# Turning the first tiles uncentred through a diagonal matmul, with a new order of loads and slots, in a fused attention and two-layer network kernel

## The chip, the cores and the metric

One core of a Trainium2 chip. The metric is the device time of one execution in microseconds (us), median of several runs. All runs quoted here are in the fast state, with a mean granted TensorE clock of 0.991 or more. A profile's span is about 1.8 us shorter than the time of the same run (288.8 against 290.5 before the change), so spans are compared with spans and times with times. Engines: PE is the tensor engine, DVE the vector engine, ACT the scalar engine, POOL GpSimd, SP the sync engine, which here only issues transfers.

## The reference

Per batch (8) and head (8): `kv = kᵀ v`, `o = q kv`, normalised by its root mean square over the 64 columns of the head. The heads are laid side by side, which gives rows `x` of 512. Then a layer norm without shift, two matrix products with a relu between, and a residual:

```python
kv  = np.einsum('bhsd,bhse->bhde', k, v)
out = np.einsum('bhsd,bhde->bhse', q, kv)
rms = np.sqrt(np.mean(out * out, axis=-1, keepdims=True) + 1e-06)
x   = (out / rms * g_norm)                       # then to (batch, 576, 512)
xn  = (x - mu) / np.sqrt(var + 1e-06) * g_ln
y   = x + np.maximum(xn @ w_ch1, 0.0) @ w_ch2    # 512 -> 2048 -> 512
```

Inputs are float32, and the kernel computes its products in bf16. The factor 1/sqrt(var) is applied after the second product, which a relu allows. So a tile can enter the network as soon as its *centred* rows have been turned (transposed).

## The kernel before

The network's two products keep PE busy (131.6 and 129.1 of its 280.9 us). Everything else (k-v products, o, norms, turns) is planned into numbered *slots*: a slot is a group of about 16 matmuls of the first product, or 4 of the second, and `at(slot, fn)` issues work just ahead of it. In the traces below each engine works in the order of issue: a copy that is issued behind another operation on DVE also runs behind it (58.60 us, behind one of 57.93, in wait 2 below). A slot number therefore also fixes the place of an instruction in the queues of DVE, ACT and SP.

```python
def turn_q_dma(b):                     # q of a batch: reorder on DVE, turn by a DMA
    q_p = kv_in.tile([128, JJ, H, D], bf16, tag="qp", bufs=2)
    nc.vector.tensor_copy(q_p.rearrange("p j h d -> p h j d"), q_in[b % NB])
    q_t = qt_pool.tile([128, JJ, HP, 128], bf16, tag="qt", name="qt")
    nc.sync.dma_start_transpose(...)
    qts[b] = q_t

def kv_of(b):                          # 40 small matmuls, then two read-outs on ACT
    kv_ps = ps_m.tile([128, HP, D], f32, tag="misc", name="kv_ps")   # ps_m: ONE buffer
    ...
    nc.scalar.copy(kvp[:D, :, :D], kv_ps[:D])
    nc.scalar.copy(kvp[D:, :, D:], kv_ps[D:])

def turn(self, on_pe):                 # a tile's centred rows (xc) into xT
    if on_pe:
        tp = ps_m.tile([128, nK, 128], bf16, tag="misc", name="tp")  # the same buffer
        ...
    else:
        nc.sync.dma_start_transpose(dst, self.xc_t)

def plan_tile(s, make, turn_at, on_pe):
    at(s, first)          # o on PE, its square on ACT, the reduction on DVE
    at(s + 2, second)     # y, x, xc on DVE
    at(s + 6, third)      # variance on ACT
    at(turn_at, fourth)

# ... cut ... batch 1's tiles turn on PE, batch 2's by DMA
for j, s, tn in ((0, 24, 30), (1, 27, 34), (2, 31, 38), (3, 35, 42)):
    plan_tile(s, lambda j=j: main_tile(1, j), tn, True)
at(36, lambda: kv_of(2))
at(36.9, lambda: turn_q_dma(2))
for j, s, tn in ((0, 45, 51), (1, 49, 55), (2, 53, 61), (3, 57.5, 64)):
    plan_tile(s, lambda j=j: main_tile(2, j), tn, False)
```

At the start, batch 0's tiles 0 and 1 are centred in halves on DVE and then turned on PE:

```python
for c, xc in enumerate(halves_xc(0)):
    half_turn(0, c, xc, nc.scalar.copy)
t[1].red()
t[1].x_g()
xc1 = list(halves_xc(1))
```

## Time and profile before

| | before |
|---|---|
| time, median of the 4 runs beside the change | 290.5 us (290.46 to 290.83) |
| span of the profiled run | 288.8 us |
| PE busy | 280.9 us, 97% |
| network's first matmul | 14.95 us |
| last matmul | 284.86 us |

The waits of PE; the columns are what waited, for what, total us, how often, the longest. In this list a 0.2 us wait for a turned tile is the only one after batch 0:

```profile
PE even L225 <- DMA v_in<-in_v_dram: 1.5, 1, 1.5
PE p L198 <- DVE eps_sb L137: 1.2, 1, 1.2
PE tp L554 <- DVE xc L547: 0.4, 1, 0.4
PE p L413 <- DMA xT_blk<-xc: 0.2, 1, 0.2
```

Second, the timeline of 54 to 63 us, where k-v and q of batch 2 are made ready (start, length, engine, line, operation):

```profile
54.37 0.36 ACT L249 CAST kv_pack<-kv_ps 64x256 bf16<-64x256 f32 x1
...
55.45 0.82 DVE L203 COPY q_p<-q_in 128x2560 bf16<-128x2560 bf16 x1
...
55.76 0.39 PE L348 MATMUL tp<-identity,xc 128*128 128x128 bf16 x4
...
56.30 3.09 SPq L205 DMA_TRANSPOSE qt<-q_p  x1
...
62.45 0.39 PE L271 MATMUL o_ps<-kv_pack,qt 128*128 128x128 bf16 x4
```

ACT frees the single buffer at 55.1, before PE wants it at 55.76. The turn of q, issued at 56.30, lands at 61.18 (4.88 us) by the landing record, and PE uses it at 62.45. **There is 0.6 us of slack on the first and 1.3 us on the second, and no view prints slack.** It has to be read by setting two starts side by side.

The page's list of DMA queues (packets, MB, share of the 16 engines).

```profile
q1 hardware_dynamic: 38480, 17.91, 31.2%
q10 hardware_dynamic: 512, 0.72, 0.7%
q8 instruction: 18, 0.29, 0.4%
```

### The profile page before, as it was taken

The numbers are of one execution on the slowest core, as the hardware profiler recorded it, in microseconds if no ns is written. First come the engines' busy times: TensorE is split into PE (matmuls) and PEld (weight loads), VectorE is DVE, ScalarE is ACT, GpSimd is POOL, SyncE is SP. The second block draws the span as 40 slices with busy tenths as digits, with TensorE's granted clock in tenths as the row PEclk, the third lists the DMA queues.
The fourth block names the chain that finished last, engine by engine and source line by source line (L and its number), as shares of the span: only waits on it lengthen the run. The fifth ranks groups of instructions, "written<-read, shape, count | busy, mean of one in ns | idle before, by whom it ended". The sixth has DMA issues, their size and how long they took to land.

```text
span 288.8 us, 5753 instructions
## 1 busy us (share of the span) xinstructions
PE 280.9 (97%) x2295; PEld 157.9 (55%) x2295; DVE 149.8 (52%) x331; ACT 153.2 (53%) x333; POOL 41.0 (14%) x69
## 2 busy tenths in 40 slices
PE   7889999999999999999999999999999999999994
PEld 3579756995479644444444444444444444444444
DVE  5774119938897783764376935762578200220022
ACT  3477844985379733872288318921893066016400
POOL 8522510041005004100500032000000000000000
PEclk9999999999999999999999999999999999999999
DMA  7999999979788959996994189947203410230033
GB/s 214 199 206 205 198 190 195 214 112 193 138 173 101 194 108 157 202 159 120 157 217 68 39 152 219 155 84 149 56 18 64 101 36 0 48 81 19 0 73 75
DMA packets 67546, 36.76 MB, mean 127 GB/s; under 512 B 35516, under 2 KB 62524, under 8 KB 67520
## 3 DMA queue, kind: packets, MB, share of 16 engines
q0 software_dynamic: 28528, 17.76, 43.8%
q1 hardware_dynamic: 38480, 17.91, 31.2%
q10 hardware_dynamic: 512, 0.72, 0.7%
q8 instruction: 18, 0.29, 0.4%
q14 instruction: 8, 0.07, 0.1%
HBM read 36.71 MB, written 9.44 MB: 160 GB/s over the span
## 4 chain that ended last, share of the span: by engine, by line
PE 85%; DMA 5%; DVE 5%; ACT 2%; issue 1%; SPq 1%; DVEq 0%; POOLq 0%
PE p L413 41%; PE p L429 37%; PE o_ps L271 2%; DMA v_in<-in_v_dram 2%; DMA qt<-q_p 2%; PE kv_ps L246 2%; DMA xT_blk<-xc 1%; DVE ss L298 1%; ACT m L416 1%; DVE x_blk L322 1%; DVE y L303 1%; DVE o_sb L434 1%; PE p L198 1%; SPq L205 1%; ACT rms L308 0%
## 5 line engine op out<-in xcount | busy, mean ns | idle before, releaser
L413 PE MATMUL p<-xT_blk,w_sb 128*128 128x128 bf16 (+2 forms) x1024 | 131.6, 286 | 0.6 <-DMA xT_blk<-xc 0.2
L429 PE MATMUL p<-w_sb,m 128*128 128x512 bf16 (+2 forms) x608 | 129.1, 368 | 0.0
L416 ACT ACTIVATE m<-p 128x512 bf16<-128x512 f32 x144 | 85.2, 596 | 43.0 <-PE p L413 40.5
L413 PEld LDWEIGHTS <-w_sb 128*128 128x128 bf16 x1024 | 78.7, 98 | 44.9 <-issue 1.5
L429 PEld LDWEIGHTS <-m 128*128 128x128 bf16 x608 | 57.0, 98 | 62.0
L434 DVE SCALAR_TENSOR_TENSOR o_sb<-p,rstd,x_blk 128x512 f32<-128x512 f32 (+2 forms) x38 | 27.3, 720 | 52.2 <-PE p L429 41.2
L277 ACT ACTIVATE sq<-o_ps 128x512 f32<-128x512 f32 x35 | 20.9, 596 | 41.7 <-PE o_ps L271 41.7
L298 DVE TENSOR_REDUCE ss<-sq 128x8 f32<-128x512 f32 x35 | 23.7, 678 | 13.0 <-ACT sq L277 12.9
L340 ACT ACTIVATE dev<-x_blk,st_blk 128x512 f32<-128x512 f32 x36 | 25.7, 714 | 6.2 <-DVE st_blk L326 6.1
L332 DVE SCALAR_TENSOR_TENSOR xc<-x_blk,st_blk,g_ln_sb 128x512 bf16<-128x512 f32 x34 | 25.6, 752 | 1.2
L303 DVE TENSOR_TENSOR y<-o_ps,inv 128x512 f32<-128x512 f32 x33 | 22.8, 692 | 3.4 <-PE p L413 0.5
L322 DVE SCALAR_TENSOR_TENSOR x_blk<-y,g_norm_sb 128x512 f32<-128x512 f32 x33 | 22.8, 692 | 1.1
L315 DVE RECIPROCAL inv<-rms 128x8 f32<-128x8 f32 x36 | 7.2, 201 | 23.0 <-ACT rms L308 23.0
L422 DVE RECIPROCAL rstd<-rstd 128x4 f32<-128x4 f32 x9 | 1.6, 175 | 31.2 <-ACT rstd L421 31.1
L308 ACT ACTIVATE rms<-ss,eps_sb 128x8 f32<-128x8 f32 x36 | 10.7, 296 | 11.5 <-DVE ss L298 11.4
L98 POOL COPY gate<-qt 1x1 bf16<-1x1 bf16 x5 | 0.9, 177 | 106.4 <-DMA qt<-q_p 106.4
L271 PEld LDWEIGHTS <-qt 128*128 128x128 bf16 (+1 forms) x156 | 10.2, 100 | 8.1 <-issue 1.7
L271 PE MATMUL o_ps<-kv_pack,qt 128*128 128x128 bf16 (+1 forms) x156 | 13.7, 220 | 0.2
L198 PE MATMUL p<-fill_sb 128*128 128x512 bf16 x27 | 8.0, 448 | 1.2 <-DVE eps_sb L137 1.2
L340 ACT ACTIVATION_READ_ACCUMULATOR dev<-x_blk,st_blk 128x1 f32 x36 | 6.8, 189 | 0.0
L249 ACT CAST kv_pack<-kv_ps 64x256 bf16<-64x256 f32 x7 | 2.6, 366 | 7.7 <-PE kv_ps L246 7.7
L246 PEld LDWEIGHTS <-k_in 128*64 128x64 bf16 x280 | 5.0, 112 | 2.6 <-issue 2.5
(80 smaller groups left out, 110.5 us busy)
## 6 DMA issues: line engine op xcount, KB each, us to landing
out_dram<-o_sb SPq DMA_DIRECT2D x70, 128.0 KB, 2.4
w_sb<-in_moe_w_ch_dram POOLq DMA_DIRECT2D x8, 512.0 KB, 15.2
q_in<-in_q_dram POOLq DMA_DIRECT2D x7, 320.0 KB, 12.3
k_in<-in_k_dram POOLq DMA_DIRECT2D x7, 320.0 KB, 6.0
v_in<-in_v_dram POOLq DMA_DIRECT2D x7, 320.0 KB, 8.6
q_in<-in_q_dram POOLq DMA_DIRECT2D x8, 256.0 KB, 12.3
k_in<-in_k_dram POOLq DMA_DIRECT2D x7, 256.0 KB, 6.7
v_in<-in_v_dram POOLq DMA_DIRECT2D x7, 256.0 KB, 10.6
```

What stands on the lines that cost most here:

```text
L198: nc.tensor.matmul(p1, lhsT=fill_sb[:, :128], rhs=fill_sb, start=True, stop=True)
L271: nc.tensor.matmul(flat[rows, hp * 128:(hp + 1) * 128], lhsT=lhsT_of(hp), rhs=kvp[:, hp, :], start=True, stop=True)
L277: nc.scalar.activation(self.sq_t, self.o_ps, func=AF.Square)
L298: nc.vector.tensor_reduce(self.ss, self.sq_t, axis=AX.X, op=ALU.add)
L303: nc.vector.tensor_mul(self.y_t, self.o_ps, self.inv().to_broadcast([128, H, D]))
L322: nc.vector.scalar_tensor_tensor(x_blk[:, ts].rearrange("p (h d) -> p h d", h=H), in0=self.y_t, scalar=1.0, in1=g_norm_sb.to_broadcast([12 ...
L332: nc.vector.scalar_tensor_tensor(self.xc_t, in0=x_blk[:, self.ts], scalar=st[:, 1, self.ts:self.ts + 1], in1=g_ln_sb, op0=ALU.add, op1=ALU ...
L340: nc.scalar.activation(dev, x_blk[:, ts], func=AF.Square, bias=st[:, 1, ts:ts + 1], accum_out=st[:, 2, ts:ts + 1])
L413: nc.tensor.matmul(p1[:, i, :], lhsT=w1_sb[:, kk, de * 128:(de + 1) * 128], rhs=blk[2][:, kk, sl], start=(kk == 0), stop=(kk == nK - 1))
L416: nc.scalar.activation(m1[:, de0:de0 + per, sl], p1, func=AF.Relu)
L429: nc.tensor.matmul(p2[:, c0:c1], lhsT=m1s[b][:, de, ts * 128:(ts + 1) * 128], rhs=w2_sb[:, de, c0:c1], start=(de == 0), stop=(de == nDe - 1))
L434: nc.vector.scalar_tensor_tensor(o_sb[:, c0:c1], in0=p2[:, c0:c1], scalar=rstds[b][:, ts:ts + 1], in1=blks[b][0][:, ts, c0:c1], op0=ALU.mu ...
```

## The change

Its intent is to let PE enter the network's second stage earlier. Tiles 0 and 1 of batch 0 are turned before they are centred: a second matmul with the constant -1/512 and a diagonal of the row sums subtracts the mean in PSUM, and the layer norm's gain rides on the copies out. Tile 2's q and o go ahead of tile 1's turn. The upper half of q's rows is loaded in two pieces and w2 in five. The slots of batches 2, 3 and 4 are renumbered to suit; those of batch 1's main tiles and of batches 5 to 7 stay (`x_at` below equals the old `s + 2`). Cut to its core:

```diff
-    nc.gpsimd.dma_start(q_in[0][64:, :, :J], up(q, 0))
+    nc.gpsimd.dma_start(q_in[0][64:, :, :2], up(q, 0)[:, :, :2])
     load_w1(1)
     load_w1(2)
+    nc.gpsimd.dma_start(q_in[0][64:, :, 2:J], up(q, 0)[:, :, 2:])
     load_w1(3)
 ...
+        def turned(kk):
+            nc.tensor.matmul(tps[kk // 2][:, kk % 2], lhsT=flat[:, kk * 128:(kk + 1) * 128],
+                             rhs=identity, start=True, stop=False)
+
+        def centred(kk):
+            nc.tensor.matmul(tps[kk // 2][:, kk % 2], lhsT=mean_sb, rhs=self.diag,
+                             start=False, stop=True)
 ...
-    for c, xc in enumerate(halves_xc(0)):
-        half_turn(0, c, xc, nc.scalar.copy)
+    t[0].x_b()
+    t[0].mean_b(True)
     t[1].red()
-    t[1].x_g()
-    xc1 = list(halves_xc(1))
+    ...
+    t[0].turn_b()
+    turn_first(2, ps_m, "misc")
+    t[1].x_b()
+    t[1].mean_b()
 ...
-    for j, s, tn in ((0, 24, 30), (1, 27, 34), (2, 31, 38), (3, 35, 42)):
-        plan_tile(s, lambda j=j: main_tile(1, j), tn, True)
+    for j, s, x_at, tn in ((0, 24, 26, 30), (1, 27, 29, 34), (2, 31, 33, 38), (3, 35, 37, 42)):
+        plan_tile(s, lambda j=j: main_tile(1, j), tn, True, x_at)
-    at(36, lambda: kv_of(2))
-    at(36.9, lambda: turn_q_dma(2))
-    for j, s, tn in ((0, 45, 51), (1, 49, 55), (2, 53, 61), (3, 57.5, 64)):
+    at(37, lambda: kv_of(2))
+    at(37.8, lambda: turn_q_dma(2))
+    for j, s, tn in ((0, 46, 52), (1, 50, 56), (2, 54, 61), (3, 58, 64.5)):
 ...
+    for b, at_load, at_kv, at_q, at_o, step in (
+            (3, 48, 57, 57.7, 67, 4.7), (4, 68, 86, 87.3, 98.5, 4.5), ...
```

More of the change, by code (lines that the diff above doesn't have):

```diff
@@ L107, in load_w1, with load_w2 @@
             w1_sb[:, :, sl], moe_w_ch1[:, sl].rearrange("(ko p) n -> p ko n", p=128))
-    def load_w2(c):
-        n = nDe // 4
+    def load_w2(de0, de1):
         nc.gpsimd.dma_start(
-            w2_sb[:, c * n:(c + 1) * n, :],
-            moe_w_ch2[c * n * 128:(c + 1) * n * 128, :].rearrange("(ko p) n -> p ko n", p=128))
+            w2_sb[:, de0:de1, :],
+            moe_w_ch2[de0 * 128:de1 * 128, :].rearrange("(ko p) n -> p ko n", p=128))
     def pairs(t, hp0, hp1):
@@ L122 @@
     gate = consts.tile([1, 1], bf16)
+    mean_sb = consts.tile([128, 128], bf16)
+    gl_rows = consts.tile([nK, 128], f32)
+    four_sb = consts.tile([nK, nK], f32)
+    g_lnT_sb = consts.tile([128, nK], f32)
+    nc.vector.memset(mean_sb, -1.0 / Dm)
     nc.vector.memset(fill_sb, 0.0)
@@ L148 @@
                 ap=[[0, 4], list(g_norm.ap[0])]))
+    nc.sync.dma_start(gl_rows, bass.AP(tensor=moe_g_ln.tensor, offset=moe_g_ln.offset,
+                                       ap=[[128, nK], [1, 128]]))
     nc.vector.memset(kv_pack[0], 0.0)
@@ L155 @@
         nc.vector.memset(t, 0.0)
-    load_w2(0)
-    load_w2(1)
+    load_w2(0, 4)
+    load_w2(4, 8)
     for dst, src in ((q_in, q), (k_in, k), (v_in, v)):
         load(dst[1], src, 1)
-    load_w2(2)
-    load_w2(3)
+    load_w2(8, 10)
+    load_w2(10, 12)
+    load_w2(12, nDe)
     qts, held, blks, rstds, m1s, q_ps = {}, {}, {}, {}, {}, {}
@@ L284, in o_g, with x_b, mean_b @@
                                  rhs=kv_g[:, hp, :], start=True, stop=True)
-        def x_g(self):
+        def x_b(self):
+            _, st, _ = self.blk
+            self.i = self.inv().to_broadcast([128, H, D])
+            self.xb = work.tile([128, H, D], bf16, tag="xc", bufs=4, name="xb")
+            nc.vector.scalar_tensor_tensor(
+                self.xb, in0=self.og_ps, scalar=1.0, in1=self.i, op0=ALU.mult, op1=ALU.mult,
+                accum_out=st[:, 0, self.ts:self.ts + 1])
+        def mean_b(self, on_act=False):
+            self.diag = work.tile([128, 128], bf16, tag="diag", name="diag")
+            total = self.blk[1][:, 0, self.ts:self.ts + 1]
+            if on_act:
+                nc.scalar.activation(self.diag, identity, func=AF.Copy, scale=total)
+            else:
+                nc.vector.tensor_scalar_mul(self.diag, identity, total)
@@ new lines, in turn_b @@
+        def turn_b(self):
+            ts = self.ts
+            flat = self.xb.rearrange("p h d -> p (h d)")
+            tps = [ps_out.tile([128, 2, 128], f32, tag="ops", name="tp") for _ in range(2)]
+            def turned(kk):
[4 more added lines that the diff above has]
+                                 start=False, stop=True)
+            turned(0)
+            turned(2)
+            for kk in range(0, nK, 2):
+                centred(kk)
+                turned(kk + 1)
+                centred(kk + 1)
+            dst = self.blk[2][:, :, ts * 128:(ts + 1) * 128]
+            for kk in range(2):
+                nc.scalar.activation(dst[:, kk], tps[kk // 2][:, kk % 2], func=AF.Copy,
+                                     scale=g_lnT_sb[:, kk:kk + 1])
+            nc.vector.tensor_mul(dst[:, 2:], tps[1],
+                                 g_lnT_sb[:, 2:].rearrange("p (k o) -> p k o", o=1)
+                                 .to_broadcast([128, 2, 128]))
+            del self.xb, self.diag
@@ L287, in x_g @@
+        def x_g(self, mean=False):
             x_blk, st, _ = self.blk
             ts = self.ts
-            nc.vector.scalar_tensor_tensor(
-                x_blk[:, ts].rearrange("p (h d) -> p h d", h=H), in0=self.og_ps, scalar=1.0,
-                in1=self.inv().to_broadcast([128, H, D]), op0=ALU.mult, op1=ALU.mult,
-                accum_out=st[:, 0, ts:ts + 1])
+            x = x_blk[:, ts].rearrange("p (h d) -> p h d", h=H)
+            if mean:
+                self.i = self.inv().to_broadcast([128, H, D])
+                nc.vector.scalar_tensor_tensor(
+                    x, in0=self.og_ps, scalar=1.0, in1=self.i, op0=ALU.mult, op1=ALU.mult,
+                    accum_out=st[:, 0, ts:ts + 1])
+            else:
+                nc.vector.tensor_mul(x, self.og_ps, self.i)
@@ L293, in x_g @@
             nc.vector.tensor_scalar_mul(st[:, 1, ts:ts + 1], st[:, 0, ts:ts + 1], -1.0 / Dm)
-            del self.og_ps
+            del self.og_ps, self.i
         def red(self):
@@ L369, in rem_tile, with plan_tile @@
         return Tile(mms, blks["rem"], b // 2)
-    def plan_tile(s, make, turn_at, on_pe):
+    def plan_tile(s, make, turn_at, on_pe, x_at=None):
         box = []
@@ L393, in plan_tile @@
         at(s, first)
-        at(s + 2, second)
+        at(x_at or s + 2, second)
         at(s + 6, third)
@@ L426, in mm2_part @@
         for de in range(de0, de1):
-            if de % 4 == 0:
+            if (de - de0) % 4 == 0 and (de1 - de0 > 2 or ts % 2 == 0):
                 tick()
@@ L483 @@
     del gl_row
+    nc.vector.tensor_copy(four_sb, identity[:nK, :nK])
     qts[0] = qt_pool.tile([128, JJ, HP, 128], bf16, tag="qt", name="qt")
@@ L489 @@
     kv_b = KvFirst(HP - 1, HP, ((ps1, "p1"), (ps1, "p1")))
-    t = [main_tile(0, 0)] + [main_tile(0, i, *((ps1, "p1") if i == 1 else (ps2, "p2")))
+    t = [main_tile(0, 0)] + [main_tile(0, i, *((ps1, "p1"), (ps_m, "misc"), (ps2, "p2"))[i - 1])
                              for i in range(1, 4)]
@@ L536, with before_6 @@
     t[1].o_g(ps1, "p1")
-    fill(5, dead)
+    fill(1, dead)
+    glT = ps1.tile([128, nK], f32, tag="p1", name="glT")
+    nc.tensor.matmul(glT, lhsT=gl_rows, rhs=four_sb, start=True, stop=True)
+    fill(1, dead)
     del dead
-    t[0].x_g()
-    def halves_xc(i):
-        x_blk, st, _ = t[i].blk
-        for c in range(2):
-            cs = slice(c * Dm // 2, (c + 1) * Dm // 2)
-            xc = work.tile([128, Dm // 2], bf16, tag="xch", bufs=4, name="xc")
-            nc.vector.scalar_tensor_tensor(xc, in0=x_blk[:, i, cs], scalar=st[:, 1, i:i + 1],
-                                           in1=g_ln_sb[:, cs], op0=ALU.add, op1=ALU.mult)
-            yield xc
-    def half_turn(i, c, xc, copy):
-        tp = ps_out.tile([128, 2, 128], bf16, tag="ops", name="tp")
-        for kk in range(2):
-            nc.tensor.transpose(tp[:, kk, :], xc[:, kk * 128:(kk + 1) * 128], identity)
-        copy(t[i].blk[2][:, 2 * c:2 * c + 2, i * 128:(i + 1) * 128], tp)
-    for c, xc in enumerate(halves_xc(0)):
-        half_turn(0, c, xc, nc.scalar.copy)
-    t[1].red()
-    t[1].x_g()
-    xc1 = list(halves_xc(1))
+    t[0].x_b()
+    t[0].mean_b(True)
+    t[1].red()
+    nc.vector.tensor_copy(g_lnT_sb, glT)
+    del glT
+    t[1].root()
+    t[0].turn_b()
+    turn_first(2, ps_m, "misc")
+    t[1].x_b()
+    t[1].mean_b()
     def before_1():
-        turn_first(2, ps_m, "misc")
-        tp = ps2.tile([128, HP, 128], bf16, tag="p2", name="tp")
-        turn_groups(tp, 3, 0, H)
-        half_turn(1, 0, xc1[0], nc.scalar.copy)
         t[2].o()
-        half_turn(1, 1, xc1[1], nc.vector.tensor_copy)
+        t[1].turn_b()
         t[2].sq()
-        nc.scalar.copy(qts[0][:, 3], tp)
+        t[0].x_g()
         t[2].red()
         t[2].root()
-        del tp, xc1[:]
     def before_2():
         t[2].o_g(ps2, "p2")
-        t[2].x_g()
+        t[2].x_g(True)
         t[2].xc()
-    def before_5():
+        t[1].x_g()
+    def before_6():
         t[3].o()
@@ L596 @@
     at(2, before_2)
-    at(5, lambda: t[2].turn(True))
-    at(5.1, before_5)
+    at(5, lambda: (turn_first(3, ps_out, "ops", nc.vector.tensor_copy), t[2].turn(True)))
+    at(6, before_6)
     at(9.5, next_loads)
@@ L602 @@
         at(16 + i, lambda i=i: t[i].var())
-    at(20, lambda: (rstd_of(0), t.clear()))
+    at(20.3, lambda: (rstd_of(0), t.clear()))
     def q_start():
@@ L617, in q_turns @@
         del q_ps[1]
-    at(14.5, q_start)
-    at(19, q_turns)
+    at(15.6, q_start)
+    at(20, q_turns)
     at(22, lambda: kv_of(1))
-    for j, s, tn in ((0, 24, 30), (1, 27, 34), (2, 31, 38), (3, 35, 42)):
-        plan_tile(s, lambda j=j: main_tile(1, j), tn, True)
+    for j, s, x_at, tn in ((0, 24, 26, 30), (1, 27, 29, 34), (2, 31, 33, 38), (3, 35, 37, 42)):
+        plan_tile(s, lambda j=j: main_tile(1, j), tn, True, x_at)
     at(46, lambda: rstd_of(1))
-    at(36, lambda: kv_of(2))
-    at(36.9, lambda: turn_q_dma(2))
-    for j, s, tn in ((0, 45, 51), (1, 49, 55), (2, 53, 61), (3, 57.5, 64)):
+    at(37, lambda: kv_of(2))
+    at(37.8, lambda: turn_q_dma(2))
+    for j, s, tn in ((0, 46, 52), (1, 50, 56), (2, 54, 61), (3, 58, 64.5)):
         plan_tile(s, lambda j=j: main_tile(2, j), tn, False)
-    plan_tile(62, lambda: rem_tile(1), 69, False)
+    plan_tile(62.5, lambda: rem_tile(1), 69, False)
     at(78, lambda: rstd_of(2))
-    for b in range(3, B):
-        s = 32 * b
-        at(47 if b == 3 else s - 60,
-           lambda b=b: load_batch(b, qts[b - 1][:1, J, HP - 1, 127:],
-                                  *([blks[2][2][:1, nK - 1, 511:]] if b == 4 else [])))
-        d = -41 if b == 3 else -45
-        at(s + d + (1 if b < 5 else 0), lambda b=b: kv_of(b))
-        at(s + d + 1.7, lambda b=b: turn_q_dma(b))
+    for b, at_load, at_kv, at_q, at_o, step in (
+            (3, 48, 57, 57.7, 67, 4.7), (4, 68, 86, 87.3, 98.5, 4.5),
+            *((b, 32 * b - 60, 32 * b - 45, 32 * b - 43.3, 32 * b - 32, 5) for b in range(5, B))):
+        at(at_load, lambda b=b: load_batch(b, qts[b - 1][:1, J, HP - 1, 127:],
+                                           *([blks[2][2][:1, nK - 1, 511:]] if b == 4 else [])))
+        at(at_kv, lambda b=b: kv_of(b))
+        at(at_q, lambda b=b: turn_q_dma(b))
         for j in range(J):
-            o = s + d + (11 if b == 3 else 13) + 5 * j
+            o = at_o + step * j
             plan_tile(o, lambda b=b, j=j: main_tile(b, j), o + 6, False)
         if b % 2:
-            plan_tile(s - 14, lambda b=b: rem_tile(b), s - 8, False)
-        at(s + 14, lambda b=b: rstd_of(b))
+            o = 32 * b - (12 if b == 3 else 14)
+            plan_tile(o, lambda b=b: rem_tile(b), o + 6, False)
+        at(32 * b + 14, lambda b=b: rstd_of(b))
     at(32 * B + 14, lambda: rstd_of("rem"))
@@ L654 @@
     p2s += [ps2.tile([128, Dm], f32, tag="p2", name="p2") for _ in range(2)]
-    for de0, de1 in ((0, nDe // 2), (nDe // 2, nDe * 3 // 4)):
+    for de0, de1 in ((0, 8), (8, 10), (10, 12), (12, nDe)):
         for ts in range(4):
-            mm2_part(0, ts, p2s[ts], de0, de1)
-    for ts in range(4):
-        p2 = p2s[ts]
-        p2s[ts] = None
-        mm2_part(0, ts, p2, nDe * 3 // 4, nDe)
-        finish(0, ts, p2)
-        del p2
+            p2 = p2s[ts]
+            mm2_part(0, ts, p2, de0, de1)
+            if de1 == nDe:
+                p2s[ts] = None
+                finish(0, ts, p2)
+            del p2
     del blks[0], m1s[0]
```

## The prediction

> **What bounds the kernel now.** I began with the page: busy times, slices, waits of the tensor engine (PE).
>
> ```profile
> PE 280.9 (97%) x2295; PEld 157.9 (55%) x2295; DVE 149.8 (52%) x331; ACT 153.2 (53%) x333; POOL 41.0 (14%) x69
> ...
> PE   7889999999999999999999999999999999999994
> ...
> DMA  7999999979788959996994189947203410230033
> ...
> L413 PE MATMUL p<-xT_blk,w_sb 128*128 128x128 bf16 (+2 forms) x1024 | 131.6, 286 | 0.6 <-DMA xT_blk<-xc 0.2
> ```
>
> PE is never idle for long after slice 4 (7.2 us each). No change can gain much unless it removes PE work, and this one removes next to none. So I looked for places where PE starts a matmul later than the one before allows. The chain of waits shows three clusters.
>
> First, batch 0's tiles 0 and 1, until their two-layer network can run:
>
> ```profile
> 13.10 1.08 PE p L198 x5
> ...
> 14.52 0.37 ACT xT_blk L555
> 14.92 0.37 ACT xT_blk L555
> ...
> 16.76 0.50 DVE xc L547
> ...
> 17.30 0.29 PE tp L554 x2
> ...
> 18.36 0.94 PE p L413 x14
> ...
> 24.57 0.30 ACT rms L308
> 24.87 0.49 ACT m L416
> ...
> 25.41 2.85 PE p L413 x48
> ```
>
> Columns: start, length, what. Five filler matmuls, then mean, centring in halves, transposes and copies; tile 1's turn is waited for; a relu (L416) behind a square root costs 0.24 us more near 25 us.
>
> Second, the first v of batch 1. The timeline shows it in GpSimd's and PE's rows:
>
> ```profile
> 39.00 0.68 POOL L94 DMA_DIRECT2D q_in<-in_q_dram  x1 [1.88 <-DMA v_in<-in_v_dram]
> ```
>
> GpSimd issued nothing until v had landed; the landing record of that transfer says 38.47 us. PE starts the k-v products of batch 1 at 38.72. Following on its matmul of 38.39 without a wait would be 38.39 + 0.213 (512 columns) + 0.096 (the usual switch between these shapes, seen at batches 3 to 6) = 38.70. So v and PE arrive within 0.03 us of each other. **This decides what the head start is worth.**
>
> Third, the border of batches 2 and 3:
>
> ```profile
> 105.65 0.82 DVE L203 COPY q_p<-q_in 128x2560 bf16<-128x2560 bf16 x1
> ...
> 106.53 3.10 SPq L205 DMA_TRANSPOSE qt<-q_p  x1
> ...
> 109.69 1.26 SPq L352 DMA_TRANSPOSE xT_blk<-xc  x1
> ...
> 111.63 0.40 PE L271 MATMUL o_ps<-kv_pack,qt 128*128 128x128 bf16 x4
> ...
> 112.25 1.02 PE L413 MATMUL p<-xT_blk,w_sb 128*128 128x512 bf16 x4 [0.23 <-DMA xT_blk<-xc]
> ```
>
> The sync queue issues the turn of batch 4's q (3.10 us) ahead of the turn of batch 3's last tile, whose xc was ready at 102.4. PE waits for both: from start to start, [...] 0.27 us ahead of L271 and 0.40 ahead of L413.
>
> [...] x48 in 2.69 us is 56 ns, x12 in 2.59 us is 216. [...] batch 0's loads and weights land one after another, 13.3 to 44.8 us, at 199 to 207 GB/s in every 4 us stretch from 8 to 36 us. [...] 128x512 from PSUM takes 0.69 us.
>
> **The change part by part.**
>
> *Diagonal turn, tiles 0 and 1.* Removed per tile: the -mean (0.15 us), two half centrings (0.88), four transposes, two copies of 128x256 (0.37 each). Added per tile: a 128x128 diagonal (estimate from the 128x256 and 128x512 copies, 0.37 and 0.59: 0.26 us on the scalar engine, ACT[...]), eight matmuls of 56 ns, two ACT copies of 128x128 (0.26 each), one DVE product of 128x256 (0.37). Worked through: the uncentred tile 0 is there at 13.43, diagonal 13.75, eight matmuls end 14.3. But ACT then does tile 1's root (waits for the reduction, 14.15) 14.2 to 14.5 and the two copies, to 15.0. PE meanwhile turns q's third group, which needs the first half of the upper q: landing 13.31 (w1's first quarter) + half of the 2.31 us that the whole took = about 14.5. So the network's first matmul comes at 15.0 to 15.3; it was 14.95, with a further gap to 15.34. **No gain on tile 0**, though q's third turn (0.48 us with its switches) is already behind.
> Tile 1: uncentred 15.7, diagonal 15.95, matmuls to 16.7; its copies wait for tile 0's relu (16.1 to 16.7) and end 17.2. Its 16 matmuls end at about 18.15 against 19.14: 1.0 us ahead, of which 0.48 is q's fourth turn, put off to slot 5.
>
> *Debt.* x itself is needed for variance and residual, so two 0.69 us products return on DVE. Tile 0's stands ahead of tile 2's reduction, so tile 2's root ends at 18.96, its relu behind at 19.5, and PE, ready at 19.3, loses 0.3. Tile 3's o, now one slot later with its q copied by DVE, avoids most of the 0.24 us at 25.11.
> Head start at the second product's first slot: 1.0 - 0.48 - 0.3 + 0.2 = 0.4 us at best, 0.1 to 0.2 less if upper q's half lands late.
>
> *At batch 1's v.* The bytes ahead of v are the same, less none, plus 2 KB of g. Unless the halves load faster, v lands at 38.47 again and the 0.2 to 0.4 us become a wait: **worth 0 to 0.1.**
>
> *w2's third quarter in two pieces.* It landed at 41.475, 81 ns of excess ahead of PE's 41.52; half of it lands about 1.5 us sooner: gain 0.07.
>
> *Later slots.* The instruction order of the changed kernel has batch 3's last turn ahead of batch 4's q turn on the sync queue, and batch 4's first o 2.5 slots later (two matmul slots of 0.86 us). q, ready by about 112.0, then meets a PE that needs it at about 112.8. Both gaps close: 0.27 + 0.40 = 0.67, less some 0.04 of switches: 0.63. At 82.79 PE waited 0.21 for batch 3's q (landed 83.06); the copy of q moves one slot, but DVE's o_sb now fills two of its 0.37 us waits for the square root, so q is ready nearly as early while PE needs it 0.9 us later: 0.1.
>
> Sum: 0.05 + 0.07 + 0.63 + 0.1 = 0.85; I take 0.1 to 0.15 off for a new small wait somewhere. 290.46 - 0.7 = **289.75 us**.
>
> **Rivals.** (1) *The head start counts in full*: v lands sooner because the small q pieces flow better (the whole upper q took 2.31 us for 256 KB, the same size of batch 1 1.39). Another 0.3 to 0.9 us: about 289.1. Against: the queue is full throughout. (2) *The start gets slower*: upper q's half lands after 14.6 and now stands ahead of the first slot; every 0.1 us beyond the head start of 0.3 counts fully: 290.2 to 290.6. For: landings of neighbours scatter by up to 1 us. (3) *DVE becomes the bound* in batch 2 to 4: slots begin one later, DVE is 8 to 9 tenths full there; if batch 4's q copy slips by 1 us, PE waits again at the new place and the 0.63 shrink to 0.2: 290.2. Against: batch 3's tiles stand 4.7 slots apart (over 4 us), DVE had idle moments at 95 us (1.28).
>
> **Range and chances.** All terms are tenths of 290 us; 2% is 5.8 us, more than every wait named here together. Range 289.1 to 290.7; faster by over 2% 0.01, within 0.98, slower 0.01.
>
> **What would show it.** The first 128x128 matmul of L471 (was L413) near 15.1, tile 1's last near 18.2; a wait on DMA v_in ahead of the k-v products near 38.7, unchanged in time; no gap for xT_blk near 111; q's turn for batch 4 behind the tile's turn on the sync queue. Wrong if k-v of batch 1 starts over 0.3 us before 38.7 (rival 1) or after it (rival 2), or if PE still waits for qt near 113.

Its sum came to 0.05 + 0.07 + 0.63 + 0.1 = 0.85 us, and 0.7 after the allowance. An estimate for a diagonal on DVE came from no trace (it took 0.25 us after the change). That a new order of loads leaves v's landing in place was not shown beforehand; the result bore it out (38.47 us before, 38.49 after). The 0.27 and 0.40 us are given as *excess*, defined with the waits below, in which 512 columns count 0.213 us. The 0.04 of switches is the author's estimate. The 1.5 us for half of w2's quarter is half of the 3.0 us from v's landing (38.47) to the quarter's own (41.48). The scatter of landings is read off the same trace: up to 55 us, pieces of 256 KB landed 1.30 to 2.55 us after the load before them.

## The result, and the profile after

| | before | after |
|---|---|---|
| time, median of 4 runs | 290.5 us (290.46 to 290.83) | 293.8 us (293.39 to 294.26) |
| ratio of the fast runs | | 1.0112 (95%: 1.0092 to 1.0131) |
| span of the profiled run | 288.8 us | 291.6 us |
| last matmul | 284.86 us | 287.65 us |

Ratios here and below are the mean time of one kernel's fast runs over that of the other's in the same rounds, so not quite the ratio of the medians. The change made the kernel 1.1% slower, with every run outside the predicted range of 289.1 to 290.7. The page's PE row now has an 8 that was a 9 (the ninth digit, 58 to 66 us):

```profile
PE 281.0 (96%) x2302; PEld 158.4 (54%) x2302; DVE 150.3 (52%) x335; ACT 153.9 (53%) x334; POOL 43.3 (15%) x71
...
PE   8889999989999999999999999999999999999994
```

To place the loss I took from each trace the first matmul of every stage of the network (P1 is the first product, P2 the second), and from the differences the length of each stage:

| stage | before, us | after, us | difference |
|---|---|---|---|
| up to the first matmul of batch 0's P1 | 14.95 | 15.53 | +0.58 |
| P1 of batch 0 | 18.03 | 17.54 | -0.49 |
| P2 of batch 0 | 16.11 | 16.01 | -0.10 |
| **P1 of batch 1** | **16.27** | **19.14** | **+2.87** |
| P2 of batch 1 | 15.79 | 15.79 | 0.00 |
| P1 of batch 2 | 14.86 | 15.43 | +0.57 |
| P2 of batch 2 | 16.24 | 15.38 | -0.86 |
| P1 of batch 3 | 14.48 | 14.71 | +0.23 |
| the rest, to the last matmul | 158.13 | 158.12 | -0.01 |
| sum | 284.86 | 287.65 | +2.79 |

The start, where the change does its work, comes out even: +0.58 - 0.49 - 0.10 = -0.01. The border of batches 2 and 3 gains 0.63. **The loss is in P1 of batch 1, where only slot numbers changed**, and 0.57 more in P1 of batch 2. The busy times of that stretch, before and then after (stretch, its length, busy time of PE, PEld, DVE, ACT and POOL with their instruction counts, clock, DMA share, GB/s), say that PE stood idle there, at full clock (1.00 in both), with the same amount of work on DVE and ACT:

```profile
49.00:65.40 16.40, 16.40 (x319) 16.16 (x317) 10.46 (x22) 14.10 (x33) 3.86 (x7) 1.00 0.89 168
```

```profile
49.00:68.20 19.20, 16.71 (x318) 16.18 (x316) 10.53 (x22) 14.29 (x32) 1.68 (x4) 1.00 0.63 129
```

PE's waits after the change:

```profile
PE o_ps L279 <- DMA qt<-q_p: 1.8, 1, 1.8
...
PE tp L406 <- ACT kv_pack L258: 0.7, 1, 0.7
PE p L471 <- ACT m L474: 0.6, 1, 0.6
PE tp L192 <- DMA q_in<-in_q_dram: 0.6, 1, 0.6
```

Below I give waits as *excess*: the time from one matmul's start to the next one's, less its columns at the pace of the trace. In before, undisturbed matmuls of 512 columns start 216 ns apart (12 in 2.59 us) and those of 128 columns 56 ns apart (48 in 2.69 us), so 384 columns more take 160 ns, and 512 count 213 ns. By this measure a start that waits for nothing has an excess of 3 ns, or about 100 at some switches (96 to k-v). It is a little more than what the list above says. The first two, in the timeline:

```profile
54.93 0.68 DVE L356 TENSOR_REDUCE ss<-sq 128x8 f32<-128x512 f32 x1
...
55.64 0.30 ACT L366 ACTIVATE rms<-ss,eps_sb 128x8 f32<-128x8 f32 x1
...
55.85 0.35 ACT L257 CAST kv_pack<-kv_ps 64x256 bf16<-64x256 f32 x1
...
56.63 0.38 PE L406 MATMUL tp<-identity,xc 128*128 128x128 bf16 x4 [0.67 <-ACT kv_pack L258]
...
57.93 0.75 DVE L390 SCALAR_TENSOR_TENSOR xc<-x_blk,st_blk,g_ln_sb 128x512 bf16<-128x512 f32 x1
...
58.60 0.82 DVE L211 COPY q_p<-q_in 128x2560 bf16<-128x2560 bf16 x1
...
59.45 3.06 SPq L213 DMA_TRANSPOSE qt<-q_p  x1
```

**Wait 1 (0.84 us).** k-v of batch 2, one slot later, starts at 54.13 (before: 53.20). Its read-outs now queue on ACT behind a variance and a square root and run from 55.85 (before: 54.37). The turn of batch 1's tile needs the same single PSUM buffer, and PE stands.

**Wait 2 (1.99 us).** The copy of batch 2's q on DVE, moved from slot 36.9 to 37.8, has crossed slot 37, where y, x and xc of batch 1's last tile are issued. It runs behind them, at 58.60 instead of 55.45. The turn is issued 3.15 us later, lands at 66.16, and batch 2's first o waits. The chain of waits (start, length, what) runs exactly through these steps:

```profile
58.60 0.83 DVE q_p L211
59.45 6.71 DMA qt<-q_p
66.16 0.05 issue
66.20 0.40 PE o_ps L279 x4
```

The turn took 6.71 us; the same turn took 4.88 before. That 1.83 us is as important as the late issue: at its usual length the turn would have landed at 59.45 + 4.88 = 64.33, and PE was ready at about 64.2.

**Wait 3 (0.79 us).** The page calls it a wait of L471 for a relu (ACT m L474). The timeline at 92 us shows what it was:

```profile
92.22 0.47 POOL L98 COPY gate<-xT_blk 1x1 bf16<-1x1 bf16 x1 [6.63 <-DMA xT_blk<-xc]
92.23 1.03 PE L471 MATMUL p<-xT_blk,w_sb 128*128 128x256 bf16 x8 [0.62 <-ACT m L474]
```

GpSimd waits for the turned last tile of batch 2 (xT) to gate a load. It gets it at 92.22, and PE starts 0.01 us later on the same tile: the wait is the turn's, and the relu named is only the last of PE's other conditions. This turn was issued at 87.57 and so took 4.65 us; before, issued at 85.71, it was there at 88.36, after 2.65 us.

So two turns took about 2 us longer than the same ones before. What lies in their time is in the packet records of the DMA queues: queue 8, "instruction", moves one packet of 16,384 bytes 18 times in each of the two profiles, on average 246 recorded matmuls and weight loads of PE apart (some records can be missing). One of them starts at 64.13 us and takes 0.93 us, 2.0 us ahead of the landing of q's turn, and one starts at 90.05. Before, they started at 62.17 and 89.20, each about 1 us after the turn had landed. This gave the theory that the experiments test.

The start: PE's first eight new matmuls end at 14.56, and then it waits for the first piece of upper q, which landed at 15.11 us:

```profile
14.34 0.22 PE L321 MATMUL tp<-diag,mean_sb 128*128 128x128 bf16 x1
...
15.16 0.44 PE L192 MATMUL tp<-identity,q_in 64*64 64x64 bf16 x16 [0.60 <-DMA q_in<-in_q_dram]
...
15.53 0.68 PE L471 MATMUL p<-xT_blk,w_sb 128*128 128x128 bf16 x9
```

And the border of batches 2 and 3: the tile's turn now stands ahead of q's on the sync queue, and no wait is left there.

```profile
107.75 1.29 SPq L410 DMA_TRANSPOSE xT_blk<-xc  x1
110.72 3.05 SPq L213 DMA_TRANSPOSE qt<-q_p  x1
```

### The profile page after: what moved, and what is told of

The parts are those of the page before. It is cut to its first block, busy times and chain, and to the rows that moved or that the text cites. A ratio compares the mean times of both kernels' runs of the same rounds, so it can differ in the third digit from the quotient of the medians.

```text
span 291.6 us, 5773 instructions
## 1 busy us (share of the span) xinstructions
PE 281.0 (96%) x2302; PEld 158.4 (54%) x2302; DVE 150.3 (52%) x335; ACT 153.9 (53%) x334; POOL 43.3 (15%) x71
## 4 chain that ended last, share of the span: by engine, by line
PE 82%; DMA 6%; DVE 5%; ACT 3%; POOL 1%; issue 1%; DVEq 0%; POOLq 0%
PE p L487 41%; PE p L471 37%; DMA q_in<-in_q_dram 3%; PE o_ps L279 2%; DMA qt<-q_p 2%; PE kv_ps L254 2%; ACT m L474 1%; DVE x_blk L380 1%; DVE y L361 1%; DVE ss L356 1%; DVE o_sb L492 1%; DVE xc L390 1%; ACT sq L285 1%; ACT rms L366 0%; POOL v_in L130 0%
## 5 line engine op out<-in xcount | busy, mean ns | idle before, releaser
L471 PE MATMUL p<-xT_blk,w_sb 128*128 128x128 bf16 (+2 forms) x1024 | 131.6, 286 | 1.0 <-ACT m L474 0.6
L474 ACT ACTIVATE m<-p 128x512 bf16<-128x512 f32 x144 | 85.2, 596 | 50.1 <-PE p L471 48.2
L471 PEld LDWEIGHTS <-w_sb 128*128 128x128 bf16 x1024 | 78.5, 98 | 45.2 <-issue 1.4
L480 DVE RECIPROCAL rstd<-rstd 128x4 f32<-128x4 f32 x9 | 1.6, 175 | 36.9 <-ACT rstd L479 36.9
L254 PE MATMUL kv_ps<-v_in,k_in 128*64 128x64 bf16 x280 | 5.8, 197 | 0.0
```

Source lines behind the costliest of these rows:

```text
L254: nc.tensor.matmul(kv_ps[hh * D:hh * D + D, hp, :], lhsT=k_in[b % NB][:, h, j, :], rhs=v_in[b % NB][:, h, j, :], start=(j == 0), stop=(j = ...
L471: nc.tensor.matmul(p1[:, i, :], lhsT=w1_sb[:, kk, de * 128:(de + 1) * 128], rhs=blk[2][:, kk, sl], start=(kk == 0), stop=(kk == nK - 1))
L474: nc.scalar.activation(m1[:, de0:de0 + per, sl], p1, func=AF.Relu)
```

## The experiments

**Theory A**: the loss comes from two slot numbers of batch 2, k-v (36 to 37) and q's copy (36.9 to 37.8); the new start is worth about nothing. **Rival**: the loss comes from the new start (more work on DVE, new loads), or from k-v alone. **Theory E**: a turn by DMA that an instruction packet falls into lands about 2 us late, and where the packets fall depends on how many instructions PE has executed. Its rival is that those turns were slowed by the loads beside them.

| kernel | what it is | median (range), us | ratio to before |
|---|---|---|---|
| after | | 293.8 (293.39 to 294.26) | 1.0112 |
| q_back | after, batch 2's q copy at its old slot | 291.1 (290.56 to 291.52) | 1.0016 (0.9999 to 1.0033) |
| kv_back | after, batch 2's k-v at its old slot | 294.01 (293.88 to 294.07) | 1.0116 (1.0101 to 1.0131) |
| kvq_back | both | 290.1 (289.7 to 290.54) | 0.9982 (0.9966 to 0.9998) |
| front_only | new start and loads, all later slots old | 291.99 (291.79 to 292.19) | 1.0047 (1.0032 to 1.0062) |
| before_split | before, 32 PE instructions more | 291.81 (291.61 to 292.35) | 1.0034 (1.0016 to 1.0053) |
| before_period | before, 252 more | 291.78 (291.25 to 292.65) | 1.0044 (1.0021 to 1.0066) |
| after_shift | after, 150 more | 291.85 (291.18 to 292.82) | 1.0035 (1.0017 to 1.0054) |
| late_only | before, batch 3's tile spacing, its remainder tile and batch 4's slots as in after | 290.18 (289.88 to 291.14) | 0.9986 (0.9964 to 1.0009) |
| late_kv23 | late_only, batch 1's k-v a slot later | 290.04 (289.89 to 290.59) | 0.9984 (0.9969 to 0.9999) |
| kvq_swap | kvq_back, upper q's first piece ahead of w1 | 289.69 (289.27 to 289.95) | 0.9962 (0.9945 to 0.998) |
| kvq_swap_kv23 | kvq_swap, batch 1's k-v a slot later | 289.37 (289.23 to 290.03) | 0.9957 (0.9939 to 0.9976) |

Every kernel gave the reference's result, with 4 runs each. They ran in three groups, each beside its own 7 runs of before (medians 290.54, 290.5 and 290.62).

### Undoing the two slot numbers: q_back, kv_back, kvq_back

```diff
-    at(37, lambda: kv_of(2))
-    at(37.8, lambda: turn_q_dma(2))
+    at(36, lambda: kv_of(2))            # kv_back, kvq_back
+    at(36.9, lambda: turn_q_dma(2))     # q_back, kvq_back
```

> The changed kernel, with only the DVE copy of batch 2's q (and its DMA turn) put back from slot 37.8 to 36.9, so that it again stands ahead of y, x and xc of batch 1's tile 3; k-v of batch 2 stays at slot 37. Theory A (that place in DVE's order is the loss): the copy starts near 55.5 us instead of 58.6, the turn lands 61 to 62, PE's wait of 1.99 us for qt near 64 is gone, the 0.84 us behind the k-v copies stays: 291.8 us. Rival B (a slot's shift of everything, or a fetch of instructions that happens to meet the turn): the wait stays, 293.5 to 294.

> The changed kernel, with only k-v of batch 2 put back from slot 37 to 36; q's copy stays late. Theory A: PE no longer waits 0.84 us at the turn of slot 38 (the PSUM buffer that k-v and that turn share is read out a slot earlier), but it then comes to batch 2's first o 0.84 us earlier and waits that much longer for q, which lands as before near 66.1: 293.7 us, worth 0.1 at most. Rival B (the two waits are separate and add): 293.0 us.

> The changed kernel, with both put back (k-v of batch 2 at slot 36, its q at 36.9), tiles of batch 2 to 4 and the start as changed. Theory A: both waits are gone, 0.84 + 1.99 us: 290.9 us, and lower by up to 0.6 if the wait of 0.79 us near 91 goes too. Rival B: no less than 293.

In q_back the copy of q is back in its place and the wait for q is gone. Wait 1 remains as it was (0.83 us). Its timeline:

```profile
55.51 0.82 DVE L211 COPY q_p<-q_in 128x2560 bf16<-128x2560 bf16 x1
...
56.36 3.06 SPq L213 DMA_TRANSPOSE qt<-q_p  x1
56.62 0.38 PE L406 MATMUL tp<-identity,xc 128*128 128x128 bf16 x4 [0.67 <-ACT kv_pack L258]
```

Moving k-v alone back removes wait 1 (the turn starts at 55.72 in kv_back) and gains nothing by the end. PE arrives earlier at the wait for q, which grows from 1.99 to 2.51 us:

```profile
55.72 0.39 PE L406 MATMUL tp<-identity,xc 128*128 128x128 bf16 x4
...
59.32 0.82 DVE L211 COPY q_p<-q_in 128x2560 bf16<-128x2560 bf16 x1
...
60.17 3.65 SPq L213 DMA_TRANSPOSE qt<-q_p  x1
65.82 0.40 PE L279 MATMUL o_ps<-kv_pack,qt 128*128 128x128 bf16 x4 [2.34 <-DMA qt<-q_p]
```

So wait 2 takes back 0.52 of the 0.84 us, not all of it as expected: P2 of batch 1 begins at 67.84, 0.38 ahead of after. That rest is lost at wait 3, which grows from 0.79 to 1.78 us and has an instruction packet in its turn:

```profile
PE o_ps L279 <- DMA qt<-q_p: 2.3, 1, 2.3
PE p L471 <- DMA xT_blk<-xc: 1.6, 1, 1.6
```

With both back, the time is 290.1, 3.7 us below after. **Theory A holds**: one digit for q is worth 2.7 us (293.8 to 291.1), and the one for k-v 1.0 us once q is out of the way (291.1 to 290.1), but nothing before, with wait 3 mixed in. In the profiles P1 of batch 1 shrinks by 2.00 us in q_back and by 0.87 more in kvq_back, as A has it; wait 3 is 0.45 us in q_back and 0.66 in kvq_back, at 88.59. Kvq_back's four runs fall into two pairs, 289.7 and 290.5, and the profiled one is of the slower pair, so what makes the faster pair faster isn't shown. Two waits in a row need not add: here the second absorbed more than half of the first.

### The new start alone: front_only

Here the new start and the w2 pieces stay, and everything from slot 14 on is as before.

> Only the change of the start (diagonal turn, tile 2 ahead of tile 1, upper q in halves, w2 in smaller pieces); every slot from 14 on as in the kernel before. Theory A (the start as such neither gains nor loses, since q's half lands at 15.1 and v of batch 1 at 38.5): 290.5 us, k-v of batch 1 near 38.75. Rival C (the start itself costs, by the later first slot of 0.58 us): 291.0. Rival D (the start gains): 290.1.

The expectation of 290.5 missed by 1.5 us. It was right about the start: k-v of batch 1 begins at 38.62 (before: 38.72), and P1 of batch 2 at 81.04 (before: 81.15). But then comes a wait of 1.35 us that neither A nor its rival knows, at 88.59, for the turned last tile of batch 2, which was issued at 85.61 (before: 85.71):

```profile
90.03 0.18 POOL L98 COPY gate<-xT_blk 1x1 bf16<-1x1 bf16 x1 [6.78 <-DMA xT_blk<-xc]
90.04 3.65 PE L471 MATMUL p<-xT_blk,w_sb 128*128 128x256 bf16 x32 [1.18 <-DMA xT_blk<-xc]
```

The turn took 4.42 us instead of 2.65, with an instruction packet at 87.02 in its middle. The same slots and almost the same times, but seven more matmuls in the program: this is where theory E comes from.

### Moving the instruction packets: before_split, before_period, after_shift

PE runs 18 dummy matmuls of 512 columns at the start. Splitting them adds PE instructions without adding columns, and nothing else in the program changes:

```diff
-        for _ in range(n):
-            nc.tensor.matmul(p1, lhsT=fill_sb[:, :128], rhs=fill_sb, start=True, stop=True)
+        for i in range(n):
+            parts = 8 if i < eighths else 2 if i < eighths + halves else 1
+            w = 512 // parts
+            for c in range(0, 512, w):
+                nc.tensor.matmul(p1[:, c:c + w], lhsT=fill_sb[:, :128], rhs=fill_sb[:, c:c + w], ...)
-    fill(18)
+    fill(18, halves=16)              # before_split:  16 matmuls and 16 weight loads more
+    fill(18, eighths=18)             # before_period: 126 and 126 more
+    fill(18, eighths=10, halves=5)   # after_shift:   75 and 75 more
```

> The kernel before, with 16 of the 18 filler matmuls at its very start (512 columns each, on zeros, while k and v load) written as two of 256 columns: the same array time, 32 more PE instructions, nothing else. Theory E (a 16 KB packet of PE's own instructions, one per some 250 of them, [...] 14 more instructions moved it from just after batch 2's last turn, 89.2 us, to into it): the packet comes near 87 to 88 us, that turn lands 1 us late or more, PE waits 0.5 to 1.4 us near 89: 291.0 to 291.9 us. Rival F (that wait comes from the changed schedule or from DVE): 290.5 us, no wait near 89.

> The kernel before, with all 18 filler matmuls of its start written as eight of 64 columns: 252 more PE instructions[...], the same columns. Theory E (what counts is where in the work the packets of instructions fall, not how many instructions there are): they fall nearly where they fell in the kernel before, the one near 89 us after batch 2's last turn; no wait of 1 us near 89 as with 32 more instructions: 290.5 us (290.2 to 290.9). Rival (more instructions cost as such, or the split of the fillers did it): 291.8 or more.

> The changed kernel as it is, with 150 more PE instructions by splitting fillers at the start, so that the packet that fell at 64.1 us into the turn of batch 2's q comes some 4 us sooner, ahead of most of that turn's data. Theory E plus A: the turn still starts near 59.4 (q's copy is as late as in the change) but takes 4.9 to 5.2 us instead of 6.7, lands near 64.4, and PE waits 0.2 to 0.5 us for it instead of 1.99: 292.2 us, plus or minus what the other packets do. Rival (the late copy alone makes the wait): the turn lands at 66.1 and 293.8 stays.

*before_split* made the kernel before 1.3 us slower with 32 instructions. Its packet at 89.20 came at 86.94, into the turn issued at 85.48. PE waits 1.00 us for it:

```profile
85.48 5.15 SPq L356 DMA_TRANSPOSE xT_blk<-xc  x3
...
89.57 3.67 PE L417 MATMUL p<-xT_blk,w_sb 128*128 128x256 bf16 x32 [0.83 <-DMA xT_blk<-xc]
89.64 0.18 POOL L98 COPY gate<-xT_blk 1x1 bf16<-1x1 bf16 x1 [6.52 <-DMA xT_blk<-xc]
```

The same late tile gates the loads of batch 4, whose v then makes PE wait another 1.73 us at 100.7 (the 0.67 us of waits that before had near 111 are gone in exchange). This is what E expected, and no load or slot differs from before.

*before_period* moves the packets by about one whole period (252 instructions, against the 246 recorded ones): one falls at 89.72, after its turn (86.36 to 89.02), and there is no wait near 89. So far E holds. Its total was expected to equal before's and is 1.2 us more: at 291.78 it is the rival's number. The trace puts that loss elsewhere. In the profiled run 0.7 us is at the start (k-v of batch 1 at 39.45 instead of 38.72; the last piece of batch 0's v lands at 10.70 instead of 9.75, with a packet at 8.6 us among the loads) and no further loss follows. Whether the packet or the split of the dummies causes it, no run tells. Two of its four runs are another 1 us slower and were not profiled; what they lost stays open.

*after_shift* moves a packet out of q's turn in the kernel after. The copy of q is as late as in after, and the turn is issued 4.7 us before PE wants it, but it takes 4.84 us instead of 6.71:

```profile
60.74 3.07 SPq L217 DMA_TRANSPOSE qt<-q_p  x1
...
65.63 0.40 PE L283 MATMUL o_ps<-kv_pack,qt 128*128 128x128 bf16 x4
```

The wait of 1.99 us shrinks to 0.14; wait 1 remains (0.83), and wait 3 is gone with no packet near it. The kernel is 1.95 us faster than after by the medians, although its start is 1.1 us later, with a packet at 8.4 us among the first loads as in before_period (that the packet delays them is likely, but no run takes it away alone). Its profiled run was the slowest of its four, with a new wait of 0.78 us for batch 4's q at 115 us. **So wait 2 needed both: a copy that came 3.15 us late, and a packet in the turn it delayed.** In the kernel after, where wait 1 has already held PE up, taking away either is enough. In kv_back, without wait 1, it wouldn't be: an estimate from its trace (a turn of 4.87 us from the issue at 60.17, PE ready at about 63.3) leaves about 1.7 us of wait without any packet.

All thirteen kernels issue the same turn of batch 2's last tile, and GpSimd's gate records its landing. Sorted by when a packet starts after the issue:

| kernel | issued, us | packet starts after, us | landed after, us |
|---|---|---|---|
| front_only | 85.61 | 1.41 | 4.42 |
| before_split | 85.48 | 1.46 | 4.16 |
| q_back | 85.63 | 1.95 | 4.24 |
| kvq_back | 84.83 | 2.13 | 4.51 |
| kv_back | 88.00 | 2.22 | 4.83 |
| kvq_swap | 84.25 | 2.38 | 2.65 |
| kvq_swap_kv23 | 83.93 | 2.46 | 2.64 |
| after | 87.57 | 2.48 | 4.65 |
| late_kv23 | 85.62 | 2.66 | 2.65 |
| late_only | 86.70 | 2.69 | 2.66 |
| before_period | 86.36 | 3.36 | 2.66 |
| before | 85.71 | 3.49 | 2.65 |
| after_shift | 87.53 | none near | 2.66 |

A packet in the first 2.2 us of the turn costs it 1.5 to 2.2 us; one at 2.66 us or later, when the turn has landed, costs nothing; in between, 2.38 to 2.48 us, it went both ways. Before_split and before differ in no load, and yet one stands at the top of the table and the other near its end. The packet records answer the rival of E directly: between issue and landing of this turn, in none of the thirteen traces, is there a packet of queue 0, which carries GpSimd's loads, nor is there one in q's turn of batch 2. Loads do matter elsewhere. Of all tile turns in the thirteen traces that have a landing record of their own, the 69 that met neither a load nor an instruction packet landed after 2.41 to 2.54 us; 59 that met loads and no such packet took 2.41 to 8.22 us.

The landing itself is 16 updates of a semaphore. In after, q_back and kvq_back fifteen of them come 2.36 to 2.52 us after the issue, as in before, and one 4.1 to 4.5 us after; in q's turn of after, fifteen come at 4.98 to 5.12 us and one at 6.71. There one update of sixteen was late. In front_only, before_split and kv_back all sixteen come late (3.7 to 4.7 us).

That the packets follow PE's instructions is also shown: before_split changed nothing but PE instructions, 32 of them, and its packet at 89.20 moved to 86.94. Why a packet of 0.9 to 1.6 us (before and after) delays a turn by up to 2.2 us, no run here shows. For the longer turn of q, which took 4.82 to 5.14 us in the eight cases of before and after with neither a packet nor a load beside it, I have fewer cases: a packet 4.68 us into it cost 1.83 us (after), one 1.97 us into it 0.75 us (kv_back), and one 4.77 us into it, 0.1 us before it landed, nothing (before_split). A later q turn of before_split (issued at 134.98) took 6.40 us with a packet 4.35 us into it.

### The later slots alone: late_only, late_kv23

```diff
-    for b in range(3, B): ...
+    for b, at_load, at_kv, at_q, at_o, step in (
+            (3, 47, 56, 56.7, 66, 4.7), (4, 68, 86, 87.3, 98.5, 4.5), ...
-    at(22, lambda: kv_of(1))
+    at(23, lambda: kv_of(1))            # late_kv23 only
```

> The kernel before, with only the slots of batches 3 and 4 changed as in the change (tiles of batch 3 4.7 slots apart, its remainder tile two slots later, k-v, q turn and tiles of batch 4 about two slots later). Theory: the two waits near 111 us, 0.27 + 0.40 us, go and nothing comes: 289.85 us (289.7 to 290.0). Rival: DVE's backlog brings a new wait at batch 4's first o: 290.4 or more.

> The start of the kernel before, with the changed slots of batches 3 and 4 and with k-v of batch 1 at slot 23: everything of the best version so far (289.4 us) but the new start, its loads and the shift of batch 2. It says what the new start is worth once v of batch 1 holds nobody up. Theory: 0.4 us of head start is missing, 289.8 to 290.0. Rival (the start gives nothing, the slots give all): 289.4.

The two waits of 0.27 and 0.40 us at 111 us are gone in both. Late_only gained 0.3 us by the medians against 0.63 in the pair of profiles. In its own profiled run the start was 1.07 us late at k-v of batch 1, as batch 0's first v landed at 8.89 (before: 8.30) and its upper q at 16.07 (15.63), but the last matmul only 0.31: 0.76 gained after that point. So the gain of this part is 0.3 to 0.8 us, and the scatter of the first loads hides which.

### Towards a better kernel: kvq_swap, kvq_swap_kv23

```diff
-    load_w1(0)
     make_identity(nc, identity)
     nc.gpsimd.dma_start(q_in[0][64:, :, :2], up(q, 0)[:, :, :2])
+    load_w1(0)
 ...
-    at(22, lambda: kv_of(1))
+    at(23, lambda: kv_of(1))            # kvq_swap_kv23 only
```

> The changed kernel with batch 2's k-v and q back at slots 36 and 36.9 (290.1 us as measured), and the first half of upper q loaded ahead of the first quarter of w1 instead of behind it. Theory G (v of batch 1 is a wall): q's half lands near 13 instead of 15.1, the 0.8 us wait of PE for it near 14.3 is gone, the first slot starts near 15.2 instead of 15.6; but k-v of batch 1 stays near 38.75 behind v's landing at 38.5, with a wait there: 290.0, gain 0.15 at most. Rival H (a head start counts): 289.7.

> The same, with k-v of batch 1 one slot later (23 instead of 22), so that PE does other work until v has landed. Theory G: no wait for v any more, the head start of 0.3 to 0.5 us is kept to the end, unless batch 1's first o at slot 24 now waits for the read-out of k-v: 289.7. Rival: o waits for the read-out and nothing is gained: 290.0 or more.

With the first piece of upper q ahead of w1's first quarter the network starts at 15.22 us (kvq_back: 15.66), with a wait of about 0.3 for w1 in place of the one for q. Then PE reaches batch 1's k-v too early: 0.14 us more than the usual switch there, with v landed at 38.49. At 289.69 us the kernel came out at rival H's number, not G's, and in the profile P1 of batch 1 begins 0.29 us ahead of kvq_back's: most of the head start got past v. With k-v one slot later there is no such wait, but in that profile v had landed at 37.82, so it doesn't show that the later slot was needed. The rest of PE's waits in kvq_swap_kv23 are all in batch 0:

```profile
PE even L233 <- DMA v_in<-in_v_dram: 0.6, 1, 0.6
PE p L471 <- ACT xT_blk L332: 0.3, 1, 0.3
PE tp L406 <- DVE xc L390: 0.3, 1, 0.3
PE p L471 <- DMA w_sb<-in_moe_w_ch_dram: 0.2, 1, 0.2
```

At 289.37 us it beats both kernels. Late_kv23, with the old start and nearly the same late slots, took 290.04, 0.7 us more. But it also lacks the shift of batch 2's tiles, and the intervals of the two ratios overlap. In the two profiles the new start with its loads in this order is 0.39 us ahead at P1 of batch 1; the last matmul comes 0.55 us earlier. A warning from the table of turns: in both swap kernels a packet falls 2.4 us into the turn, at the edge of doing harm. Part of their lead over kvq_back, up to its 0.66 us of wait 3, is the luck of that place, not a merit of the load order.

## Why the prediction was wrong

**The sum lacked two terms.** It predicted 0.7 us of gain; the profiled pair shows 2.79 us of loss. Waits 1 and 2 (0.84 + 1.99 = 2.83 us, against +2.87 in that stage) stand nowhere in it. The step that failed is "Later slots". It works through batch 4's border and batch 3's q ("the copy of q moves one slot, but DVE's o_sb now fills two of its 0.37 us waits"), and never batch 2's, where k-v and q moved by one slot too. The order of instructions on DVE, known before the prediction, had the copy of q behind xc of batch 1's last tile. I looked at that order for batch 4 and not for batch 2. The runs put 2.7 us on the q digit and 1.0 on the k-v digit, wait 3 included. None of the prediction's three signs of being wrong appeared (k-v of batch 1 came 0.07 us later than before, and PE doesn't wait for q near 113): they all looked where the prediction had looked.

**"0.1 to 0.15 off for a new small wait somewhere"** stood in for all I had not worked through. The waits not named there came to 0.84 + 1.99 + 0.79 = 3.6 us. An allowance for unknown waits should be sized by the slack they would eat (here 0.6 and 1.3 us against a shift of 0.9 us or more), not by the waits seen now.

**Instruction packets were not thought of.** The page lists them, at 0.4% of the DMA engines, and I read that share as no cost. By the table of turns, one in the wrong place costs a 2.65 us turn up to 2.2 us. Wait 3 and 1.8 us of wait 2 are due to them.

**The start** was right in sum and wrong in parts. First matmul of the network: predicted 15.0 to 15.3, measured 15.53, as upper q's first piece landed at 15.11, not 14.5. Its working took half of the whole load's duration for half of the bytes; the piece took 1.81 us here, and 0.68 in front_only, where it landed at 14.42 and the first matmul came at 15.14, inside the prediction. So this miss is within the scatter of that landing. Head start at the second product: predicted up to 0.4 us, measured -0.09 (33.07 against 32.98). Tile 1's part is there in half: its last matmul starts at 18.59 against 19.09, 0.5 us ahead where the prediction had 1.0. P1 of batch 0 is 0.49 us shorter, and the late first matmul ate it.

**Batch 1's v** was right: it landed at 38.49 (before: 38.47), and k-v began at 38.79 (before: 38.72). A longer head start would have become a wait in part: in kvq_swap, 0.14 us of one.

**w2's pieces**: predicted 0.07; that stage shortened by 0.10. No run tells its share apart.

**Batches 3 and 4** were right: predicted 0.63, measured 0.86 - 0.23 = 0.63. The 0.21 us wait for batch 3's q at 82.79 is gone too, though PE arrives there 2.9 us late, so this proves little.

**The rivals**: the second, a slower start, was half true at the first matmul and repaid by 33 us. The third named DVE and a slipped q copy, which is the mechanism of wait 2, but in batch 4, where it did not happen. Chances: I gave 0.98 to within 2%, and 1.1% is within; the range was the error.

## What to carry to other kernels

When a plan's numbers move, go through **every** producer that moved: its new neighbours on its own engine's queue, and the slack between its landing and its use. A list of waits doesn't show slack, so an item without a wait today may be the next one. Waits on one path need not add: undo the first alone and a later one may take most of the gain back (0.52 of 0.84 us in kv_back). And a change of some dozen PE instructions can cost 1 us by where the instruction packets then fall (1.3 us for 32 in before_split), so before crediting or blaming an edit with a few tenths of a per cent, see whether a turn by DMA got longer with no load beside it, and shift the packets once to tell.
